# Linear attention plus routed feed-forward on one core: tiles 0 to 2 centred only, tiles 3 to 5 turned by TensorE, and the loads of x moved

## The chip, the cores and the metric

The kernel runs on one core of a Trainium2 chip. The metric is the device time of one execution in microseconds; before the change the median of three runs is 116.94 us (116.87 to 117.31). The engines are TensorE (PE, with PEld for its weight loads), VectorE (DVE), ScalarE (ACT), GpSimd (POOL) and SyncE (SP), whose queue issues most of the transfers. Every engine works through its own queue in the order in which the program was written out; they meet through semaphores.

## The reference

All arrays are bf16. x is 2048 tokens by 640.

```python
xn = _layernorm(x, axis=-1)
qkv = (xn @ wqkv)                       # 32 heads of 20
phi = lambda t: jnp.where(t > 0, t + 1, jnp.exp(t)) + 1e-6
kv = einsum("bhsd,bhse->bhde", phi(k), v);  z = phi(k) summed over s
o = (phi(q) @ kv) / (phi(q) . z + 1e-6)
A = o @ wo
r = xn @ w_r;  idx = argsort(-r)[:, :8]
y = (silu(xn[idx] @ w_gate) * (xn[idx] @ w_up)) @ w_down
B = xn, with y * sigmoid(r[idx]) added at the rows idx
return x + A + B
```

So the first thing that every token needs is its layer norm, and k, q and the routing logit r are products of the normalized token.

## The kernel before

**Tiles.** The tokens are 16 tiles of 128 (tile t is `x_sb[:, t, :]`). The normalized tile `xn[:, t, :]` has tokens on the partitions. The products k and q contract over the 640 features, so they read the turned tile `xnT`, features on the partitions, in five chunks of 128 (`kc`). The value projection is not computed for each token: the kernel sums G = xn^T phi(k) over all tiles and multiplies by the value weights once at the end.

**One tile.** `ln_stats(t)` is two BN_STATS on halves of 320 columns (lines 162 and 165), one aggregate (166), then the reciprocal root. It is two small operations on POOL, an add (168) and a power (171); for tiles 0 and 1 it is instead two activations on ACT (175, 176). `ln_scale(t)` (180, VectorE) subtracts the mean and multiplies by the root. Turning is done either by a DMA transpose issued from SP (`turn_dma`, 205), or by five TensorE transposes into a bank of PSUM (`turn_pe`, 192) and a copy out of it (`turned`, 200 on ACT or 202 on VectorE). `k_mm` (210) is ten matmuls in two halves of 320 columns; the second half has a 321st column, w_r, which gives the logit r. `k_act` (226 to 228, ACT) evicts exp, relu and the logit; `k_phi` (233, VectorE) makes phi(k) = min(exp, 1) + relu. `g_mm` (271) is five matmuls that add the tile to G.

**q.** Twenty units of 128 features by 512 tokens: `q_mm` (244), `q_act` (256, 257), `q_phi` (263). Units 0 to 4 read the turned tiles 0 to 3, units 5 to 9 the tiles 4 to 7.

**Order.** It is written out by hand and kept. SP loads the x of tiles 0 to 3 first, ACT's queue the k weights in two halves (122: chunks 0 to 2, 124: chunks 3 and 4). A memset on POOL (147) into two columns of x 4 holds back the loads after it: x 4 to 5, x 6 to 7, the q weights, x 8 to 9. Eight matmuls on zeros (291) come first on TensorE, one more later. Tiles 0 to 2 are turned by TensorE (tile 2 with VectorE's copy), tiles 3 to 15 by DMA. Each is scaled before it is turned. The x of tiles 10 to 15 is loaded in three pairs, each ahead of one DMA transpose. The column of w_r is turned by TensorE (319) and copied by ACT into `wk_sb` (320) in the middle of the k matmuls of tile 0.

**Loop.** From t = 3 to 15 a pass has k of tile t, q of unit t - 3 and G of tile t - 1 on TensorE. On VectorE it has phi of q for unit t - 4, the scaling of tile t + 3, the statistics of tile t + 4, some adds of xn to x in later passes (9 to 15), and phi of k for tile t. On POOL it has the root of tile t + 4 and one piece of the constants (`const_piece`). On SP it has the transpose of tile t + 3 and the loads of the later weights (`pieces`). After the loop come the top 8 tokens and their feed-forward, the product of the state with the output weights, the remaining q units, and the output; the change leaves all that as it is.

**Waits to know.** A transfer takes one of eight semaphores in turn, so its issue also waits for the transfer eight before it. PSUM banks 0 to 4 belong to G from its first tile on, banks 5 and 6 to k in the loop, and bank 7 to q.

## Time and profile before

| what | value |
|---|---|
| median of three runs | 116.94 us |
| the profiled execution, its own time | 117.29 us |
| its span, first to last instruction | 115.6 us |
| PE busy | 106.8 us (92%), 914 matmuls |
| VectorE busy | 83.9 us (73%) |
| ACT busy | 64.7 us (56%) |
| POOL busy | 34.3 us (30%) |
| moved by DMA | 22.20 MB, 192 GB/s on the mean |
| granted TensorE clock | 0.999 |

The times before and after are those of the whole execution; a span lies a little below. In the rows of the order of time, the first number is the start in us from the start of the span, the second the length, then the engine and the line of the kernel, what is written and what is read, and in brackets how long the engine was idle before it and what ended that. In the chain that ended last, each row is a start, a length and what the time was spent in.

### The profile page before, as it was taken

The page shows a single profiled execution, that of the slowest core. Times are in us where ns is not written, and L with a number is a line of the kernel's source. Part 1 is how long each engine was busy: PE and PEld are TensorE (multiplying, and loading weights), DVE is VectorE, ACT ScalarE, POOL GpSimd, SP SyncE. Part 2 cuts the span into 40 slices and gives each one's busy share as a digit, 9 for nine tenths or more (in the row PEclk, how much of TensorE's full clock was granted, in tenths as well). Part 3 has the DMA queues.
Part 4 walks back from the last instruction along what each step waited for, and adds up shares of the span by engine and source line. Part 5 has one row for each costly group of instructions (what it writes and reads, how often), then busy time and mean ns, then how long its engine had stood idle before and what let it go on. Part 6 is the DMA issues. An engine that isn't in the chain of part 4 may idle for free.

```text
span 115.6 us, 2496 instructions
## 1 busy us (share of the span) xinstructions
PE 106.8 (92%) x914; PEld 63.2 (55%) x922; DVE 83.9 (73%) x178; ACT 64.7 (56%) x127; POOL 34.3 (30%) x85
## 2 busy tenths in 40 slices
PE   5989996999999999999999998889799999999990
PEld 2445452555555555555555687644445666677770
DVE  0767999599998899877988976534537668695571
ACT  1558735655687555785556648896599465400000
POOL 7305357838777674500000005400060000000000
PEclk9999999999999999999999999999999999999999
DMA  3999279905998999999764995000003696984333
GB/s 95 318 381 338 60 176 161 234 2 109 281 231 228 223 368 223 347 322 243 290 227 149 257 384 186 0 0 6 0 1 72 173 330 155 317 289 169 113 113 113
DMA packets 23814, 22.20 MB, mean 192 GB/s; under 512 B 10074, under 2 KB 22522, under 8 KB 23802
## 3 DMA queue, kind: packets, MB, share of 16 engines
q1 hardware_dynamic: 21824, 19.99, 61.9%
q10 hardware_dynamic: 1834, 2.02, 5.1%
q0 software_dynamic: 144, 0.04, 0.6%
q8 instruction: 7, 0.11, 0.4%
q14 instruction: 5, 0.04, 0.1%
HBM read 14.62 MB, written 5.28 MB: 172 GB/s over the span
## 4 chain that ended last, share of the span: by engine, by line
PE 50%; DMA 15%; issue 13%; DVE 10%; POOLq 3%; SPq 3%; ACTq 1%; ACT 1%; POOL 1%; DVEq 0%
PE ps L210 16%; PE ps L271 11%; PE ps L244 11%; PE ps L756 11%; DMA wk_sb<-in_A_wqkv_dram 5%; DMA xnT<-xn 4%; DMA x_sb<-xxd 3%; DMA xxd<-y_sb,idxw 3%; POOLq L593 3%; SPq L740 3%; DVE xn L766 1%; DVE pk L233 1%; ACT spw L787 1%; DVE st L165 1%; DVE st L162 1%
## 5 line engine op out<-in xcount | busy, mean ns | idle before, releaser
L210 PE MATMUL ps<-wk_sb,xnT 128*128 128x320 bf16 (+1 forms) x160 | 25.2, 300 | 1.6 <-DMA xnT<-xn 1.1
L244 PE MATMUL ps<-xnT,wq_sb 128*128 128x512 bf16 x94 | 23.7, 379 | 0.5 <-issue 0.3
L756 PE MATMUL ps<-late,pqT 128*128 128x320 bf16 (+2 forms) x165 | 22.6, 295 | 0.0
L226 ACT ACTIVATE ek<-ps 128x640 bf16<-128x640 f32 x16 | 11.3, 704 | 19.0 <-PE ps L210 19.0
L210 PEld LDWEIGHTS <-xnT 128*128 128x128 bf16 x160 | 15.3, 98 | 11.0 <-DMA xnT<-xn 1.9
L271 PE MATMUL ps<-pk,xn 128*128 128x512 bf16 x78 | 19.8, 379 | 0.3 <-DVE pk L233 0.2
L263 DVE SCALAR_TENSOR_TENSOR pqT<-eq,rq 128x512 bf16<-128x512 bf16 x20 | 14.2, 709 | 8.0 <-ACT rq L257 7.9
L756 PEld LDWEIGHTS <-pqT 128*128 128x128 bf16 x165 | 15.6, 98 | 6.6 <-issue 0.6
L766 DVE TENSOR_TENSOR xn<-ps,x_sb 128x640 bf16<-128x640 f32 (+3 forms) x18 | 13.1, 748 | 5.5 <-PE ps L756 5.1
L233 DVE SCALAR_TENSOR_TENSOR pk<-ek,rk 128x640 bf16<-128x640 bf16 x16 | 13.3, 831 | 3.6 <-ACT rk L227 3.4
L244 PEld LDWEIGHTS <-wq_sb 128*128 128x128 bf16 x100 | 9.4, 97 | 9.5 <-issue 0.5
L256 ACT ACTIVATE eq<-ps 128x512 bf16<-128x512 f32 x20 | 12.3, 618 | 1.5 <-PE ps L244 1.5
L271 PEld LDWEIGHTS <-xn 128*128 128x128 bf16 x80 | 7.7, 98 | 9.5 <-issue 0.5
L257 ACT ACTIVATE rq<-ps 128x512 bf16<-128x512 f32 x20 | 12.3, 616 | 0.0
L171 POOL TENSOR_TENSOR rs<-rs,half 128x1 f32<-128x1 f32 x14 | 11.1, 793 | 1.1
L227 ACT ACTIVATE rk<-ps 128x640 bf16<-128x640 f32 x16 | 11.2, 697 | 0.0
L162 DVE BATCH_NORM_STATS2 st<-x_sb 128x6 f32<-128x320 bf16 x16 | 7.7, 479 | 3.6 <-DMA x_sb<-in_A_x_dram 3.6
L168 POOL TENSOR_TENSOR rs<-mv,half 128x1 f32<-128x1 f32 x14 | 5.4, 388 | 15.6 <-DVE mv L166 15.5
L594 POOL COPY xsT<-xnT 128x5 bf16 x8 | 3.0, 383 | 22.7 <-DVE gbf L672 20.5
L180 DVE TENSOR_SCALAR xn<-x_sb,mv,rs 128x640 bf16<-128x640 bf16 x16 | 7.7, 484 | 0.7 <-ACT rs L176 0.7
L165 DVE BATCH_NORM_STATS2 st<-x_sb 128x6 f32<-128x320 bf16 x16 | 7.6, 475 | 0.0
L787 ACT CAST spw<-ps 128x1024 bf16<-128x1024 f32 x5 | 4.9, 1014 | 3.7 <-PE ps L552 2.5
(121 smaller groups left out, 105.5 us busy)
## 6 DMA issues: line engine op xcount, KB each, us to landing
x_sb<-in_A_x_dram SPq DMA_DIRECT2D x6, 320.0 KB, 4.1
wg_sb<-in_B_w_gate_dram SPq DMA_DIRECT2D x5, 384.0 KB, 5.4
wu_sb<-in_B_w_up_dram SPq DMA_DIRECT2D x5, 384.0 KB, 4.1
wd_sb<-in_B_w_down_dram SPq DMA_DIRECT2D x3, 640.0 KB, 8.1
xxd<-x_sb SPq DMA_DIRECT2D x2, 640.0 KB, 3.2
out_dram<-xn SPq DMA_DIRECT2D x8, 160.0 KB, 2.1
x_sb<-xxd SPq DMA_DIRECT2D x2, 640.0 KB, 4.8
out_dram<-xn ACTq DMA_DIRECT2D x7, 160.0 KB, 2.2
```

Of the source, the lines that this page charges most:

```text
L171: nc.gpsimd.tensor_tensor(out=rs[:, 1:2], in0=rs[:, 0:1], in1=half[:, 1:2], op=ALU.pow)
L210: nc.tensor.matmul(ps[:, b + h, 0:w], lhsT=xnT[:, kc, t * P : (t + 1) * P], rhs=wk_sb[:, kc, h * HW : h * HW + w], start=(kc == 0), stop=( ...
L226: nc.scalar.activation(e[:], ps[:, b : b + 2, 0:HW], AF.Exp)
L227: nc.scalar.activation(r[:], ps[:, b : b + 2, 0:HW], AF.Relu)
L233: nc.vector.scalar_tensor_tensor(out=pk[:, t, :].rearrange("p (b f) -> p b f", b=2), in0=e[:], scalar=1.0, in1=r[:], op0=ALU.min, op1=ALU.add,
L244: nc.tensor.matmul(ps[:, b, :], lhsT=wq_sb[:, kc, m * P : (m + 1) * P], rhs=xnT[:, kc, tb * TBLK : (tb + 1) * TBLK], start=(kc == 0), stop ...
L256: nc.scalar.activation(e[:], ps[:, b, :], AF.Exp)
L257: nc.scalar.activation(r[:], ps[:, b, :], AF.Relu)
L263: nc.vector.scalar_tensor_tensor(out=pqT[:, m, tb * TBLK : (tb + 1) * TBLK], in0=e[:], scalar=1.0, in1=r[:], op0=ALU.min, op1=ALU.add,)
L271: nc.tensor.matmul(ps[:, c, :], lhsT=xn[:, t, c * P : (c + 1) * P], rhs=pk[:, t, 0:512], start=(t == 0), stop=(t == T - 1),)
L756: nc.tensor.matmul(ps[:, b, 0 : c1 - c0], lhsT=pqT[:, kc, t * P : (t + 1) * P], rhs=M_sb[:, kc, c0:c1], start=(kc == 0), stop=(kc == KC - 1),)
L766: nc.vector.tensor_tensor(out=xn[:, t, c0:c1].rearrange("p (b f) -> p b f", f=w), in0=ps[:, b : b + n, 0:w], in1=x_sb[:, t, c0:c1].rearran ...
```

## The change

The tiles 0, 1 and 2 are only centred before they are turned (`ln_centre`, subtracting the mean). The copies put them into unused parts of `GT` (`cT`), k is computed from them, and the factor 1/std of each token is applied by ACT as the row scale of the three evictions in `k_act`. For q and G the same tiles are scaled in place later (`ln_scale_centred`) and turned once more, by DMA. All roots come from POOL. Tiles 3, 4 and 5 are scaled as before, but turned by TensorE with ACT's copies in place of a DMA transpose. The warm-up matmuls are six in place of eight plus one.

The load of x 3 is issued behind a memset that follows the first POOL select; the loads of x 4 to 9 and the q weights are issued behind POOL's root of tile 0; x 10 to 15 is issued in one place, after the transposes of tiles 0 to 2. The w_r column is turned first on TensorE, copied by ACT to `wrT`, and put into `wk_sb` by POOL; tile 0 takes its logit from `wrT` by five matmuls of one column. The prologue is written out further, to the q units 0 and 1 and the scaling of tile 7, and the loop begins at t = 5. There the constants' pieces start two passes later, and two weight loads are issued in a pass from the start. The statistics' pool has five buffers in place of four.

```diff
@@ -25,7 +25,8 @@
 FJ = F // 4
 YW = D // 4
 EPS_BF16 = 1.0013580322265625e-05
-N_WARM = 8
+N_WARM = 6
+CENTRED = 3
 
 BF16 = mybir.dt.bfloat16
 F32 = mybir.dt.float32
@@ -64,7 +65,7 @@
 
     big = ctx.enter_context(tc.tile_pool(name="big", bufs=1))
     small = ctx.enter_context(tc.tile_pool(name="small", bufs=1))
-    lnp = ctx.enter_context(tc.tile_pool(name="lnp", bufs=4))
+    lnp = ctx.enter_context(tc.tile_pool(name="lnp", bufs=5))
     evk = ctx.enter_context(tc.tile_pool(name="evk", bufs=2))
     evq = ctx.enter_context(tc.tile_pool(name="evq", bufs=2))
     psum = ctx.enter_context(tc.tile_pool(name="ps", bufs=1, space=bass.MemoryType.PSUM))
@@ -103,6 +104,7 @@
     xsT = sb([P, KC, H], BF16, "xsT")
     maskkv = sb([EB, 5, DB], BF16, "maskkv")
     wr_rows = sb([KC, P], BF16, "wr_rows")
+    wrT = sb([P, KC], BF16, "wrT")
     r_all = sb([P, T], BF16, "r_all")
     kvT = sb([EB, NB, DB], BF16, "kvT")
 
@@ -122,7 +124,6 @@
     nc.scalar.dma_start(wk_sb[:, 0:3, 0:D], wqkv_v[:, 0:3, D : 2 * D])
     nc.sync.dma_start(x_sb[:, 2, :], x_v[:, 2, :])
     nc.scalar.dma_start(wk_sb[:, 3:KC, 0:D], wqkv_v[:, 3:KC, D : 2 * D])
-    nc.sync.dma_start(x_sb[:, 3, :], x_v[:, 3, :])
     nc.scalar.preload_act_table_set("natural_log_exp_and_others")
 
 
@@ -132,28 +133,36 @@
     nc.gpsimd.memset(half[:, 1:2], -0.5)
     nc.gpsimd.memset(grep[:], 1.0)
 
-    def grep_rows(j):
+    def grep_rows(j, then=None):
         g = grep[32 * j : 32 * j + 32, :]
         nc.gpsimd.affine_select(
             out=g, in_=g, compare_op=ALU.is_ge, fill=0.0, base=0,
             pattern=[[1, D]], channel_multiplier=-DH,
         )
+        if then is not None:
+            then()
         nc.gpsimd.affine_select(
             out=g, in_=g, compare_op=ALU.is_ge, fill=0.0, base=DH - 1,
             pattern=[[-1, D]], channel_multiplier=DH,
         )
 
-    grep_rows(0)
-    nc.gpsimd.memset(x_sb[:, 4, 0:2], 0.0)
-    nc.sync.dma_start(x_sb[:, 4:6, :], x_v[:, 4:6, :])
-    nc.sync.dma_start(x_sb[:, 6:8, :], x_v[:, 6:8, :])
-    nc.sync.dma_start(wq_sb[:], wqkv_v[:, :, 0:D])
-    nc.sync.dma_start(x_sb[:, 8:10, :], x_v[:, 8:10, :])
+    def late_x3():
+        nc.gpsimd.memset(x_sb[:, 3, 0:2], 0.0)
+        nc.sync.dma_start(x_sb[:, 3, :], x_v[:, 3, :])
+
+    def late_x4():
+        nc.gpsimd.memset(x_sb[:, 4, 0:2], 0.0)
+        nc.sync.dma_start(x_sb[:, 4:6, :], x_v[:, 4:6, :])
+        nc.sync.dma_start(x_sb[:, 6:8, :], x_v[:, 6:8, :])
+        nc.sync.dma_start(wq_sb[:], wqkv_v[:, :, 0:D])
+        nc.sync.dma_start(x_sb[:, 8:10, :], x_v[:, 8:10, :])
+
+    grep_rows(0, late_x3)
 
 
     stat = {}
 
-    def ln_stats(t, parts="abr", root="P"):
+    def ln_stats(t, parts="ab"):
         if "a" in parts:
             st = lnp.tile([P, 2, nc.vector.BN_STATS_DIM], F32, tag="st", name=f"st{t}")
             mv = lnp.tile([P, 2], F32, tag="mv", name=f"mv{t}")
@@ -164,16 +173,25 @@
             st, mv, rs = stat[t]
             nc.vector.bn_stats(out=st[:, 1, :], in_=x_sb[:, t, HW:D])
             nc.vector.bn_aggr(out=mv[:], in_=st[:])
-            if root == "P":
-                nc.gpsimd.tensor_tensor(
-                    out=rs[:, 0:1], in0=mv[:, 1:2], in1=half[:, 0:1], op=ALU.add
-                )
-                nc.gpsimd.tensor_tensor(
-                    out=rs[:, 1:2], in0=rs[:, 0:1], in1=half[:, 1:2], op=ALU.pow
-                )
-            else:
-                nc.scalar.activation(rs[:, 0:1], mv[:, 1:2], AF.Ln, bias=half[:, 0:1])
-                nc.scalar.activation(rs[:, 1:2], rs[:, 0:1], AF.Exp, scale=-0.5)
+            nc.gpsimd.tensor_tensor(
+                out=rs[:, 0:1], in0=mv[:, 1:2], in1=half[:, 0:1], op=ALU.add
+            )
+            nc.gpsimd.tensor_tensor(
+                out=rs[:, 1:2], in0=rs[:, 0:1], in1=half[:, 1:2], op=ALU.pow
+            )
+
+    def ln_centre(t):
+        _, mv, _ = stat[t]
+        nc.vector.tensor_scalar(
+            out=xn[:, t, :], in0=x_sb[:, t, :], scalar1=mv[:, 0:1], scalar2=None,
+            op0=ALU.subtract,
+        )
+
+    def ln_scale_centred(t):
+        _, _, rs = stat[t]
+        nc.vector.tensor_scalar(
+            out=xn[:, t, :], in0=xn[:, t, :], scalar1=rs[:, 1:2], scalar2=None, op0=ALU.mult
+        )
 
     def ln_scale(t):
         _, mv, rs = stat.pop(t)
@@ -193,9 +211,15 @@
                 psb(b)[:, kc * P : (kc + 1) * P], xn[:, t, kc * P : (kc + 1) * P], ident[:]
             )
 
+    def cT(t):
+        return GT[:, 1 + t, :].rearrange("p (k f) -> p k f", f=P)
+
     def turned(t, b, eng, c0=0, c1=KC):
         src = psb(b)[:, c0 * P : c1 * P].rearrange("p (k f) -> p k f", f=P)
-        dst = xnT[:, c0:c1, t * P : (t + 1) * P]
+        if t < CENTRED:
+            dst = cT(t)[:, c0:c1, :]
+        else:
+            dst = xnT[:, c0:c1, t * P : (t + 1) * P]
         if eng == "A":
             nc.scalar.copy(dst, src)
         else:
@@ -205,11 +229,14 @@
         nc.sync.dma_start_transpose(xnT[:, :, t * P : (t + 1) * P], xn[:, t, :])
 
 
-    def k_one(t, b, kc, h):
-        w = HW + h
+    def k_lhs(t, kc):
+        return cT(t)[:, kc, :] if t < CENTRED else xnT[:, kc, t * P : (t + 1) * P]
+
+    def k_one(t, b, kc, h, w=None):
+        w = w or HW + h
         nc.tensor.matmul(
             ps[:, b + h, 0:w],
-            lhsT=xnT[:, kc, t * P : (t + 1) * P],
+            lhsT=k_lhs(t, kc),
             rhs=wk_sb[:, kc, h * HW : h * HW + w],
             start=(kc == 0), stop=(kc == KC - 1),
         )
@@ -223,9 +250,16 @@
     def k_act(t, b):
         e = evk.tile([P, 2, HW], BF16, tag="ek", name=f"ek{t}")
         r = evk.tile([P, 2, HW], BF16, tag="rk", name=f"rk{t}")
-        nc.scalar.activation(e[:], ps[:, b : b + 2, 0:HW], AF.Exp)
-        nc.scalar.activation(r[:], ps[:, b : b + 2, 0:HW], AF.Relu)
-        nc.scalar.copy(r_all[:, t : t + 1], ps[:, b + 1, HW : HW + 1])
+        src, logit = ps[:, b : b + 2, 0:HW], ps[:, b + 1, HW : HW + 1]
+        if t < CENTRED:
+            rs = stat[t][2][:, 1:2]
+            nc.scalar.activation(e[:], src, AF.Exp, scale=rs)
+            nc.scalar.activation(r[:], src, AF.Relu, scale=rs)
+            nc.scalar.activation(r_all[:, t : t + 1], logit, AF.Copy, scale=rs)
+        else:
+            nc.scalar.activation(e[:], src, AF.Exp)
+            nc.scalar.activation(r[:], src, AF.Relu)
+            nc.scalar.copy(r_all[:, t : t + 1], logit)
         kbuf[t] = (e, r)
 
     def k_phi(t):
@@ -293,8 +327,12 @@
             )
 
     warm(N_WARM)
-    ln_stats(0, root="A")
-    ln_stats(1, "a")
+    ln_stats(0)
+    late_x4()
+    nc.tensor.transpose(psb(4)[:, 0:KC], wr_rows[:], ident[0:KC, 0:KC])
+    nc.scalar.copy(wrT[:], psb(4)[:, 0:KC])
+    ln_centre(0)
+    turn_pe(0, 7)
     for b in range(5):
         nc.tensor.matmul(
             ps[0:EB, 3, b * DB : (b + 1) * DB],
@@ -302,56 +340,86 @@
             rhs=grep[0:H, b * DB : (b + 1) * DB],
             start=(b == 0), stop=True, skip_group_check=True,
         )
+    turned(0, 7, "A", 0, 2)
+    turned(0, 7, "A", 2, KC)
     nc.scalar.copy(
         maskkv[:], ps[0:EB, 3, 0 : 5 * DB].rearrange("p (b f) -> p b f", b=5)
     )
-    ln_scale(0)
-    turn_pe(0, 7)
-    warm(1)
-    turned(0, 7, "A", 0, 2)
-    turned(0, 7, "A", 2, KC)
-    ln_stats(1, "b", root="A")
-    ln_stats(2, "a")
-    ln_scale(1)
-    ln_stats(2, "b")
+    nc.gpsimd.tensor_copy(wk_sb[:, :, D : D + 1], wrT[:].unsqueeze(2))
+    ln_stats(1)
+    ln_centre(1)
     for kc in range(3):
-        k_one(0, 5, kc, 0)
-    nc.tensor.transpose(psb(3)[:, 0:KC], wr_rows[:], ident[0:KC, 0:KC])
-    nc.scalar.copy(wk_sb[:, :, D : D + 1], psb(3)[:, 0:KC].unsqueeze(2))
+        for h in range(2):
+            k_one(0, 5, kc, h, HW)
+    turn_pe(1, 7)
     for kc in range(3, KC):
-        k_one(0, 5, kc, 0)
-    turn_pe(1, 4)
+        for h in range(2):
+            k_one(0, 5, kc, h, HW)
     for kc in range(KC):
-        k_one(0, 5, kc, 1)
-    turned(1, 4, "A", 0, 2)
-    turned(1, 4, "A", 2, KC)
+        nc.tensor.matmul(
+            ps[:, 6, HW : HW + 1], lhsT=k_lhs(0, kc), rhs=wrT[:, kc : kc + 1],
+            start=False, stop=(kc == KC - 1), skip_group_check=True,
+        )
+    turned(1, 7, "A", 0, 2)
+    turned(1, 7, "A", 2, KC)
+    ln_stats(2)
+    ln_centre(2)
+    k_act(0, 5)
+    k_mm(1, 2, 0, 4)
+    turn_pe(2, 4)
+    k_mm(1, 2, 4)
+    turned(2, 4, "A", 0, 2)
+    turned(2, 4, "V", 2, KC)
+    ln_scale_centred(0)
+    turn_dma(0)
+    ln_scale_centred(1)
+    turn_dma(1)
+    k_act(1, 2)
     ln_stats(3)
-    ln_scale(2)
-    k_act(0, 5)
-    k_mm(1, 2, 0, 6)
-    turn_pe(2, 7)
-    turned(2, 7, "V")
-    k_mm(1, 2, 6)
-    k_act(1, 2)
     k_phi(0)
+    k_mm(2, 5)
     ln_scale(3)
-    turn_dma(3)
-    ln_stats(4)
-    k_mm(2, 5)
+    g_mm(0)
     k_act(2, 5)
     k_phi(1)
+    ln_scale_centred(2)
+    turn_dma(2)
+    for t0 in (10, 12, 14):
+        nc.sync.dma_start(x_sb[:, t0 : t0 + 2, :], x_v[:, t0 : t0 + 2, :])
+    turn_pe(3, 7)
+    turned(3, 7, "A", 0, 2)
+    turned(3, 7, "A", 2, KC)
+    g_mm(1)
+    ln_stats(4)
+    k_phi(2)
+    ln_scale(4)
+    k_mm(3, 5)
+    turn_pe(4, 7)
+    turned(4, 7, "A", 0, 2)
+    turned(4, 7, "A", 2, KC)
     ln_stats(5)
-    ln_scale(4)
-    nc.sync.dma_start(x_sb[:, 10:12, :], x_v[:, 10:12, :])
-    turn_dma(4)
-    g_mm(0)
-    k_phi(2)
-    g_mm(1)
+    k_act(3, 5)
+    g_mm(2)
+    ln_scale(5)
+    k_phi(3)
+    q_mm(0, 7)
     ln_stats(6)
-    ln_scale(5)
-    nc.sync.dma_start(x_sb[:, 12:14, :], x_v[:, 12:14, :])
-    turn_dma(5)
-    nc.sync.dma_start(x_sb[:, 14:16, :], x_v[:, 14:16, :])
+    ln_scale(6)
+    turn_dma(6)
+    q_act(0, 7)
+    k_mm(4, 5)
+    q_phi(0)
+    k_act(4, 5)
+    turn_pe(5, 7)
+    turned(5, 7, "A")
+    g_mm(3)
+    ln_stats(7)
+    k_phi(4)
+    ln_scale(7)
+    turn_dma(7)
+    q_mm(1, 7)
+    q_act(1, 7)
+    ln_stats(8)
 
     def const_piece(i):
         if i == 0:
@@ -431,25 +499,22 @@
 
 
     added = 0
-    for t in range(3, T):
+    for t in range(5, T):
         k_mm(t, 5)
-        if t >= 4:
-            q_phi(t - 4)
-        if t == 3:
-            ln_stats(7)
+        q_phi(t - 4)
         if t + 3 < T:
             ln_scale(t + 3)
             turn_dma(t + 3)
-        if 3 < t < T - 4:
+        if t + 4 < T:
             ln_stats(t + 4)
         for _ in range(ADDS.get(t, 0)):
             add_xn(added)
             added += 1
-        const_piece(t - 3)
-        if t >= 5:
-            for _ in range(2 if t > 6 else 1):
-                if len(pieces) > 3:
-                    pieces.pop(0)()
+        if t < 12:
+            const_piece(t - 5)
+        for _ in range(2):
+            if len(pieces) > 3:
+                pieces.pop(0)()
         if t in STORES:
             store_xx(*STORES[t])
         k_act(t, 5)
```

## The prediction

> **What bounds the kernel now.** I read the busy times by stretch first, then the waits, the chain that ended last, and the order of time of the first 20 us.
>
> ```profile
> 10.00:20.00 10.00, 8.60 (x51) 4.57 (x52) 9.42 (x23) 5.53 (x13) 5.30 (x11) 1.00 0.70 163
> 20.00:28.00 8.00, 7.95 (x48) 4.58 (x47) 6.25 (x13) 4.69 (x10) 5.23 (x12) 1.00 0.52 110
> ...
> PE ps L210 <- DMA xnT<-xn: 1.1, 1, 1.1
> ```
>
> The columns are the stretch, its length, then busy PE, PEld, DVE, ACT and POOL. From 20 us TensorE is busy without a gap. Before that VectorE is the full one: 9.42 of 10 us. The one long TensorE wait is 1.1 us for the turned tile 4. The chain says whose lateness that is:
>
> ```profile
> 1.83 5.82 DMA wk_sb<-in_A_wqkv_dram
> ...
> 8.13 0.28 PE ps L192 x5
> ...
> 13.74 0.40 DVE st L162
> 14.15 0.40 DVE st L165
> ...
> 14.57 0.21 DVE mv L166
> 14.78 0.31 DVE xn L180
> 15.12 4.55 DMA xnT<-xn
> ...
> 19.72 1.56 PE ps L210 x10
> 21.27 1.08 PE ps L244 x5
> 22.35 1.08 PE ps L271 x5
> 23.43 1.38 PE ps L210 x10
> ```
>
> First the weights (second half landed at 1.83 + 5.82 = 7.65), then VectorE's queue up to the scaling of tile 4, then its DMA transpose. From 19.72 a pass costs 1.38 (k) + 1.08 (q) + 1.08 (G) = 3.54 us, all TensorE. So only what moves the loop's start, or makes VectorE late inside it, counts; the tail is unchanged and follows.
>
> **What VectorE's steps cost.** Rows in order of time (start, length, engine, line):
>
> ```profile
> 4.04 0.21 DVE L166 BATCH_NORM_AGGREGATE mv<-st 128x2 f32<-128x12 f32 x1
> 4.92 0.45 DVE L180 TENSOR_SCALAR xn<-x_sb,mv,rs 128x640 bf16<-128x640 bf16 x1 [0.31 <-ACT rs L176]
> 6.17 0.75 ACT L200 COPY xnT<-ps 128x256 bf16<-128x256 bf16 x2 [0.28 <-PE ps L192]
> 6.60 0.69 PE L210 MATMUL ps<-wk_sb,xnT 128*128 128x320 bf16 x3 [0.17 <-ACT xnT L200]
> 9.95 0.45 PE L192 MATMUL ps<-ident,xn 128*128 128x128 bf16 x5
> 10.44 0.49 DVE L202 COPY xnT<-ps 128x640 bf16<-128x640 bf16 x1 [0.55 <-PE ps L192]
> 12.85 0.21 DVE L166 BATCH_NORM_AGGREGATE mv<-st 128x2 f32<-128x12 f32 x1
> 12.97 0.77 DVE L233 SCALAR_TENSOR_TENSOR pk<-ek,rk 128x640 bf16<-128x640 bf16 x1
> 13.21 0.59 POOL L168 TENSOR_TENSOR rs<-mv,half 128x1 f32<-128x1 f32 x1 [2.63 <-DVE mv L166]
> 13.87 0.55 POOL L171 TENSOR_TENSOR rs<-rs,half 128x1 f32<-128x1 f32 x1
> 16.45 0.70 ACT L226 ACTIVATE ek<-ps 128x640 bf16<-128x640 f32 x1 [2.52 <-PE ps L210]
> 16.66 0.21 DVE L166 BATCH_NORM_AGGREGATE mv<-st 128x2 f32<-128x12 f32 x1
> 16.95 0.28 POOL L168 TENSOR_TENSOR rs<-mv,half 128x1 f32<-128x1 f32 x1 [0.71 <-DVE mv L166]
> 17.30 0.55 POOL L171 TENSOR_TENSOR rs<-rs,half 128x1 f32<-128x1 f32 x1
> 18.44 0.82 DVE L233 SCALAR_TENSOR_TENSOR pk<-ek,rk 128x640 bf16<-128x640 bf16 x1
> 18.65 1.02 POOL L171 TENSOR_TENSOR rs<-rs,half 128x1 f32<-128x1 f32 x1
> 19.18 0.69 DVE L263 SCALAR_TENSOR_TENSOR pqT<-eq,rq 128x512 bf16<-128x512 bf16 x1
> 29.27 1.24 PE L271 MATMUL ps<-pk,xn 128*128 128x512 bf16 x5
> ```
>
> A tile's statistics, start to next start: 0.40 + 0.40 + 0.02 + 0.08 until the pipe is empty, 0.12 for the aggregate (12.85 to 12.97) = 1.02 us. Phi of k: 0.73 to the next start (18.44 to 19.18). Phi of q: 0.69 long, 0.61 to the next by the same overlap of 0.08. A scaling: 0.31 (14.78 to 15.09) before a phi; I take 0.36 before statistics, 0.45 less the overlap.
>
> The reciprocal root on POOL is the important one. Alone, it runs from 16.66 + 0.21 = 16.87 to 17.30 + 0.55 = 17.85: **0.98 us** after the aggregate. With a phi behind the statistics the add, started at 13.21, ends at 13.80, just after that phi (12.97 + 0.77 = 13.74), and the root comes at 14.42, **0.68 after the phi's end**. The power at 18.65 was held likewise, past the phi that ended at 19.26. So POOL's small operations do not finish while VectorE streams a two-input operation.
>
> Before, nearly no scaling waits for this: the loop scales tile t + 3 one pass after its statistics, and the prologue puts statistics 5 ahead of scaling 4.
>
> **The change, part by part.**
>
> *Start of tile 0.* Centring (as the scaling, 0.45) starts at the aggregate's end, 4.25, instead of 4.92: tile 0 moves up 0.67. The first k matmul goes from 6.60 to about 5.94. It lies under the weights: the last four need the second half.
>
> *Weights and x of tile 3.* The issue of x 3 moves behind a POOL select and memset, from 2.18 to about 3.45. Its packets came behind those of tile 2:
>
> ```profile
> L125 SPq DMA_DIRECT2D x_sb<-in_A_x_dram x1: 432/432/432, 2.2 to 2.2; - x1
> DMA to landing us min/median/max: 5.2/5.2/5.2
> ...
> 4.11 0.39 SPq L148 DMA_DIRECT2D x_sb<-in_A_x_dram  x1
> ```
>
> It landed at 2.18 + 5.2 = 7.4, near the weights, so little clears their way; the x of tiles 4 and 5, now behind POOL's root of tile 0 (5.4 instead of 4.11), frees some more. Bounds for the landing: 7.65 (nothing gained) and 6.9 (the 160 KB of x 3 and some of x 4 out of the way). I take 7.3. The loads of x 4 to 9 and wq slip by 1.4 us; their readers (statistics 4 at 14, q of unit 0 at 18) have more room than that.
>
> *Logit by itself for tile 0*: five one-column matmuls, which the trace does not show; between nothing and the 0.138 of a 320-column matmul each; I take 0.06, by the nearest row (a 128-column transpose, 0.28 by five), 0.3 in all. The row-scale operand in three k evictions of each of three tiles costs ACT nothing to 0.7 (a second eviction pass) each; I take 0.1, and ACT waited 19 us in all for those matmuls:
>
> ```profile
> ACT ek L226 <- PE ps L210: 19.0, 15, 2.5
> ```
>
> *PE.* k of tile 0 ends at 7.35 + 4 x 0.138 + 0.3 = 8.2, four of tile 1 at 8.75, the transposes of tile 2 (5 in 0.45) at 9.2. Only then may VectorE copy its share: it starts at **9.24**, where it used to copy at 10.44. 1.2 us are gained here.
>
> *VectorE from there* does three scalings more than before (in place, tiles 0 to 2), less 0.23 of copy, and now has each scaling right behind its own statistics, with at most a phi between. The queue, in the new order:
>
> copy 0.26, scale 0 and 1 0.72: 10.22. Statistics 3: 11.24. Phi 0, whose place also holds the root: 0.82 + 0.69 + 0.03 = 1.54, 12.78. Scale 3, phi 1, scale 2 (0.31 + 0.73 + 0.36): 14.18. Statistics 4 and phi 2 with the held root: 16.74. Scale 4 and statistics 5: 18.12. Bare root (0.98, plus 0.09 as the aggregate is 0.21 long and counted with 0.12): 19.19. Scale 5: 19.55. Then phi 3 waits for ACT: transposes of tile 4 after scale 4 (17.18) end at 17.69, their copies take 0.75 and the k eviction of tile 3 behind them two of 0.70 with 0.1 overlapped, so 19.8; phi 3: 20.53. Statistics 6, bare root: 22.62. Scale 6, phi of q 0: 23.54. Statistics 7, phi 4 with held root: 26.10. Scale 7, statistics 8: 27.48. Phi of q 1 with held root (0.69 + 0.69 + 0.03): 28.89. Scale 8, statistics 9: 30.27. Phi 5 ends at **31.09**.
>
> G of tile 5 needs phi 5: it starts at 31.14, and started at 29.27. That is **+1.87**. The 1.2 us of head start is eaten by five to six exposed roots of 0.7 to 1.0 us and 1.1 us of scalings.
>
> *What is late next.* TensorE's pass is 3.54; VectorE's late pass is 1.02 + 0.73 + 0.61 + 0.36 and a root wait of about 0.5 = 3.2, so it would catch up by 0.3 a pass, but
>
> ```profile
> 27.77 0.72 POOL L137 TENSOR_SCALAR_AFFINE_SELECT grep<-grep 32x640 bf16<-32x640 bf16 x1
> ...
> 27.84 0.84 DVE L180 TENSOR_SCALAR xn<-x_sb,mv,rs 128x640 bf16<-128x640 bf16 x1
> ```
>
> the constants' selects (three passes, now two passes later) lengthen a scaling by 0.4, and from pass 9 the adds bring 0.36. It stays late over passes 6 to 11, and I estimate one more wait of 0.3. Sum: 1.87 + 0.3 = **+2.2 us**.
>
> *Hidden at no cost.* DMA transposes of tiles 0 to 2 are issued at 10, 11 and 14.3; even at 4.55 to landing the last is there at 18.9, against q of unit 0 at 18.6, before a later wait. The six x tiles issued together go ahead of the transpose of tile 6 on SP, but by 17.3, and that transpose waits until 23 for scaling 6. The column of w_r, copied by POOL after both weight halves, holds the roots of tiles 1 and 2 to 9.5; scalings 1 and 2 come at 9.9 and 13.8. A deeper statistics pool costs nothing.
>
> The profiled execution (117.29 around a span of 115.6) lies 0.35 above the median; I add to the median: 116.94 + 2.2 = **119.1**, span near 117.8.
>
> **The rivals.**
>
> *TensorE-bound start, VectorE keeps up.* Then k starts 0.66 earlier and the wait of 1.1 goes, against three more sets of transposes (3 x 0.28) and 0.3 of logits: 1.14. That gives -0.62: 116.3. The wait row speaks for it, the 9.42 of 10 us against. Chance 0.09.
>
> *The root is not held.* If each came 0.98 after its aggregate, the three held phis would cost 1.07 instead of 1.54 and the phi of q 0.34 less: 1.75 less, +0.45, 117.4. Against it are the two held rows. [...] Chance 0.10.
>
> *The clock comes late.*
>
> ```profile
> 1.38 3.59 PE L291 MATMUL ps<-GT 128*128 128x512 bf16 x8 [1.38 <-POOL GT L129]
> 5.93 0.50 PE L291 MATMUL ps<-GT 128*128 128x512 bf16 x1
> ```
>
> Eight warm matmuls took 0.43 each, later ones of that shape 0.216; full rate came around 6 us. The change drops three and leaves TensorE idle for some 0.7 us around 4.4. [...] For it: the idle time. [...] Chance 0.09.
>
> *Holding x 3 does nothing* for the weights: landing at 7.65, +0.35 on the sum, 119.5. It belongs to the forecast's own range, 118.5 to 120.
>
> **Numbers.** Forecast 0.70, unheld root 0.10, late clock 0.09, TensorE-bound 0.09, the rest others. Within 0.5% (116.36 to 117.52, about what a measurement here can tell) lies the unheld root: 0.10; slower 0.81; faster 0.09. The range of 117.1 to 120.8 takes in the unheld root and the late clock and leaves out the fast rival.
>
> **What would show it.** VectorE idle ahead of the scalings of tiles 3 to 8, released by POOL's root, 0.7 to 1.1 us each; phi 5 ending near 31, G of tile 5 waiting for it; TensorE idle ahead of the transposes of tile 4 by about 0.8; the weights near 7.3. I am wrong if the loop's k of tile 6 starts before 26.8, or if those waits are there and G of tile 5 is not late.

## The result, and the profile after

The changed kernel took 121.2 us as the median of four executions (120.12 to 122.24), beside 117.02 us (116.87 to 117.31) for the kernel before on the same chip. The ratio is 1.0284, 95% interval 1.0248 to 1.032, which puts the change at +3.3 us against the +2.2 of the forecast; two of the five executions, the profiled one of 122.24 us among them, came out at 122 us and are not in that ratio, and what sets them apart is found below.

The waits of the profiled execution of the changed kernel, each with its total in us, how often, and the longest:

```profile
DVE xn L198 <- POOL rs L179: 7.5, 12, 1.0
DVE GT L226 <- ACT GT L224: 3.9, 1, 3.9
PE ps L305 <- DVE pk L267: 1.7, 3, 1.0
PEld L237 <- DMA xnT<-xn: 1.5, 2, 0.8
```

The first row is the forecast's mechanism: twelve scalings on VectorE now wait 7.5 us for POOL's root, where nearly none did. The second was not in the forecast: VectorE's copy of tile 2 waits for a copy by ACT.

The busy times by stretch (stretch, length, busy PE, PEld, DVE, ACT, POOL, granted clock, DMA share, GB/s):

```profile
10.00:20.00 10.00, 8.17 (x56) 4.79 (x54) 7.00 (x17) 5.65 (x13) 2.41 (x4) 1.00 0.63 163
20.00:28.00 8.00, 7.32 (x45) 4.08 (x44) 5.27 (x13) 5.93 (x13) 2.58 (x6) 1.00 0.38 118
```

From 10 to 20 us VectorE fell from 9.42 of 10 to 7.00 and is late all the same: its idle time is waiting. TensorE, which was busy for 7.95 of 8 us from 20 to 28, is busy for 7.32.

The order of time of the same execution, where the two waits stand (start, length, engine, line, and in brackets the idle time before and what ended it):

```profile
4.69 0.71 PE L210 MATMUL ps<-ident,xn 128*128 128x128 bf16 x5 [0.46 <-DVE xn L185]
...
6.01 1.76 PE L237 MATMUL ps<-wk_sb,GT 128*128 128x320 bf16 x6
...
7.08 0.20 POOL L348 COPY wk_sb<-wrT 128x5 bf16<-128x5 bf16 x1 [1.69 <-DMA wk_sb<-in_A_wqkv_dram]
...
9.58 0.79 ACT L256 ACTIVATE ek<-ps,rs 128x640 bf16<-128x640 f32 x1 [0.49 <-PE ps L359]
...
10.37 0.67 PE L210 MATMUL ps<-ident,xn 128*128 128x128 bf16 x5
10.95 0.26 ACT L258 ACTIVATE r_all<-ps,rs 128x1 bf16<-128x1 f32 x1
11.09 0.38 ACT L224 COPY GT<-ps 128x256 bf16<-128x256 bf16 x1
11.50 0.36 DVE L226 COPY GT<-ps 128x384 bf16<-128x384 bf16 x1 [3.89 <-ACT GT L224]
...
13.41 0.77 DVE L267 SCALAR_TENSOR_TENSOR pk<-ek,rk 128x640 bf16<-128x640 bf16 x1
13.57 0.66 POOL L176 TENSOR_TENSOR rs<-mv,half 128x1 f32<-128x1 f32 x1 [4.73 <-DVE mv L175]
14.31 0.55 POOL L179 TENSOR_TENSOR rs<-rs,half 128x1 f32<-128x1 f32 x1
14.89 0.45 DVE L198 TENSOR_SCALAR xn<-x_sb,mv,rs 128x640 bf16<-128x640 bf16 x1 [0.71 <-POOL rs L179]
...
20.08 0.21 DVE L175 BATCH_NORM_AGGREGATE mv<-st 128x2 f32<-128x12 f32 x1
20.43 0.19 POOL L176 TENSOR_TENSOR rs<-mv,half 128x1 f32<-128x1 f32 x1 [1.66 <-DVE mv L175]
20.70 0.55 POOL L179 TENSOR_TENSOR rs<-rs,half 128x1 f32<-128x1 f32 x1
21.29 0.45 DVE L198 TENSOR_SCALAR xn<-x_sb,mv,rs 128x640 bf16<-128x640 bf16 x1 [1.00 <-POOL rs L179]
...
33.11 1.24 PE L305 MATMUL ps<-pk,xn 128*128 128x512 bf16 x5 [0.48 <-DVE pk L267]
```

Three things are to be seen. First, the held root: the add of 13.57 takes 0.66 us and ends at 14.23, just after the phi that ended at 13.41 + 0.77 = 14.18, and the scaling follows 0.71 after the phi's end. The bare root, without a phi, takes 0.19 + 0.55 and ends at 21.25, 0.96 after its aggregate's end. Second, the copy of line 226 starts at 11.50, behind ACT's share of the same tile (11.09 to 11.47), though the transposes that it reads ended at 10.37 + 0.67 = 11.04; and in ACT's queue that share stands behind the three evictions of tile 0, which end at 11.21. Third, the k matmuls of tile 0 run at about half rate: six in 1.76 us, where the rows of before give 0.138 each, 0.83 for six. This is the forecast's late clock; the granted clock of the profile reads 1.00 from 4 to 10 us all the same, so the name rests on the lengths of the matmuls. G of tile 5 starts at 33.11; before it was 29.27.

### The profile page after: what moved, and what is told of

It reads as the page before. It is cut to its first block, busy times and chain, and to the rows that moved or that the text cites. A ratio compares the mean times of both kernels' runs of the same rounds, so it can differ in the third digit from the quotient of the medians.

```text
span 120.5 us, 2554 instructions
## 1 busy us (share of the span) xinstructions
PE 110.1 (91%) x939; PEld 65.0 (54%) x939; DVE 83.9 (70%) x181; ACT 67.0 (56%) x129; POOL 36.2 (30%) x91
## 4 chain that ended last, share of the span: by engine, by line
PE 47%; DVE 19%; DMA 10%; ACT 9%; POOL 8%; issue 4%; ACTq 1%; DVEq 0%; POOLq 0%
PE ps L821 14%; PE ps L278 10%; PE ps L237 8%; DMA xnT<-xn 6%; PE ps L305 5%; POOL rs L179 5%; POOL rs L176 4%; DMA wk_sb<-in_A_wqkv_dram 4%; DVE xn L198 4%; ACT spw L634 3%; DVE st L171 3%; DVE st L174 3%; DVE xn L831 2%; DVE mv L175 1%; PE ps L314 1%
## 5 line engine op out<-in xcount | busy, mean ns | idle before, releaser
L278 PE MATMUL ps<-xnT,wq_sb 128*128 128x512 bf16 x100 | 24.4, 379 | 0.7 <-ACT xnT L224 0.7
L237 PE MATMUL ps<-wk_sb,xnT 128*128 128x320 bf16 (+1 forms) x130 | 20.1, 300 | 0.5 <-DMA xnT<-xn 0.3
L297 DVE SCALAR_TENSOR_TENSOR pqT<-eq,rq 128x512 bf16<-128x512 bf16 x20 | 13.7, 684 | 6.2 <-ACT rq L291 6.2
L260 ACT ACTIVATE ek<-ps 128x640 bf16<-128x640 f32 x13 | 9.2, 705 | 14.3 <-PE ps L237 14.3
L237 PEld LDWEIGHTS <-xnT 128*128 128x128 bf16 x130 | 12.6, 98 | 8.4 <-DMA xnT<-xn 1.5
L176 POOL TENSOR_TENSOR rs<-mv,half 128x1 f32<-128x1 f32 x16 | 7.8, 485 | 19.9 <-DVE mv L175 19.0
L267 DVE SCALAR_TENSOR_TENSOR pk<-ek,rk 128x640 bf16<-128x640 bf16 x16 | 12.8, 799 | 0.5 <-ACT rk L261 0.4
L261 ACT ACTIVATE rk<-ps 128x640 bf16<-128x640 f32 x13 | 9.1, 700 | 0.0
```

The lines of the kernel that those rows point to most:

```text
L176: nc.gpsimd.tensor_tensor(out=rs[:, 0:1], in0=mv[:, 1:2], in1=half[:, 0:1], op=ALU.add)
L237: nc.tensor.matmul(ps[:, b + h, 0:w], lhsT=k_lhs(t, kc), rhs=wk_sb[:, kc, h * HW : h * HW + w], start=(kc == 0), stop=(kc == KC - 1),)
L267: nc.vector.scalar_tensor_tensor(out=pk[:, t, :].rearrange("p (b f) -> p b f", b=2), in0=e[:], scalar=1.0, in1=r[:], op0=ALU.min, op1=ALU.add,
L278: nc.tensor.matmul(ps[:, b, :], lhsT=wq_sb[:, kc, m * P : (m + 1) * P], rhs=xnT[:, kc, tb * TBLK : (tb + 1) * TBLK], start=(kc == 0), stop ...
L297: nc.vector.scalar_tensor_tensor(out=pqT[:, m, tb * TBLK : (tb + 1) * TBLK], in0=e[:], scalar=1.0, in1=r[:], op0=ALU.min, op1=ALU.add,)
```

## The experiments

Ratios are to the kernel before, run beside each version on the same chip, with their 95% intervals; the rows of each kernel are from one profiled execution of it. I call "the start" what lies ahead of VectorE's copy of tile 2, "the prologue" what lies from there to G of tile 5, and "the loop" the rest up to the first matmul of the state's product (line 280 before, 314 after). That matmul started at 65.09 before, and what follows it is the same work.

### The changed kernel again, twice

Nothing is edited.

> The changed kernel once more, for a second trace. All theories: about 120.3. If TensorE reaches its full rate near 6 us in this execution (the k matmuls of tile 0 in pairs of 0.14 us instead of 0.27), VectorE's copy of tile 2 starts near 9.5 instead of 11.5, and G of tile 5 near 31.3 instead of 33.1; the waits of VectorE for POOL's root before the scalings stay at 0.7 to 1.0 us each.

Measured: 121.99 us (121.67 to 122.29), 1.0403 (1.0373 to 1.0433). That is above the 120.3 expected, and all four executions lie in the upper part of the first set's scatter. In the profiled one (122.29 us) the condition for the early start did not come: the first six k matmuls of tile 0 take 1.78, VectorE's copy starts at 11.48 and G of tile 5 at 33.10, as in the first profile, and the waits for a root are 7.5 us in all again.

> The changed kernel once more, with nothing edited, for its spread. Theory (a TensorE clock that comes late in some executions and in time in others): the times fall into two groups, near 120.3 and near 122, some 1.5 us apart; in the profiled execution the first six matmuls of k of tile 0 take about 1.76 us where the time is near 122, and 1.2 or less where it is near 120.3. Rival (the scatter comes from the loads): both kinds of execution run those matmuls at the same rate, and the weights' landing, near 7.05 otherwise, differs by a microsecond or more.

Measured: 121.4 us (120.7 to 122.38), 1.0368 (1.0306 to 1.043). The six times fall into two groups with nothing between: 120.70, 120.76, 120.97 and 121.83, 121.95, 122.38, whose means (120.81 and 122.05) differ by 1.24. This time the profiled execution is one of the lower group, 120.70 us. Its order of time:

```profile
4.72 0.45 PE L210 MATMUL ps<-ident,xn 128*128 128x128 bf16 x5 [0.49 <-DVE xn L185]
...
5.95 0.98 PE L237 MATMUL ps<-wk_sb,GT 128*128 128x320 bf16 x6 [0.47 <-DMA wk_sb<-in_A_wqkv_dram]
...
7.55 0.20 POOL L348 COPY wk_sb<-wrT 128x5 bf16<-128x5 bf16 x1 [2.14 <-DMA wk_sb<-in_A_wqkv_dram]
...
8.66 0.44 PE L210 MATMUL ps<-ident,xn 128*128 128x128 bf16 x5
...
9.72 0.27 ACT L258 ACTIVATE r_all<-ps,rs 128x1 bf16<-128x1 f32 x1
9.86 0.38 ACT L224 COPY GT<-ps 128x256 bf16<-128x256 bf16 x1
...
10.28 0.36 DVE L226 COPY GT<-ps 128x384 bf16<-128x384 bf16 x1 [1.77 <-ACT GT L224]
...
18.08 0.46 PE L210 MATMUL ps<-ident,xn 128*128 128x128 bf16 x5 [0.56 <-DVE xn L198]
...
31.05 0.77 DVE L267 SCALAR_TENSOR_TENSOR pk<-ek,rk 128x640 bf16<-128x640 bf16 x1
...
31.88 1.24 PE L305 MATMUL ps<-pk,xn 128*128 128x512 bf16 x5 [0.48 <-DVE pk L267]
...
36.09 0.93 DVE L198 TENSOR_SCALAR xn<-x_sb,mv,rs 128x640 bf16<-128x640 bf16 x1 [0.44 <-POOL rs L179]
36.13 0.71 POOL L138 TENSOR_SCALAR_AFFINE_SELECT grep<-grep 32x640 bf16<-32x640 bf16 x1
...
39.79 0.93 DVE L198 TENSOR_SCALAR xn<-x_sb,mv,rs 128x640 bf16<-128x640 bf16 x1 [0.45 <-POOL rs L179]
...
46.61 1.24 PE L305 MATMUL ps<-pk,xn 128*128 128x512 bf16 x5 [0.40 <-DVE pk L267]
...
68.42 1.74 PE L314 MATMUL ps<-pk,xn 128*128 128x128 bf16 x28
```

The five transposes of tile 0 take 0.45 here, the first six k matmuls 0.98, and the copy starts at 10.28, 1.22 before that of the execution of 122.24 us, although the weights landed later (7.55 against 7.08 by the column's copy). So it is TensorE's rate and not the loads that parts the two groups: the theory of the late clock holds, its rival fails. Here the wait of the copy is ACT's queue alone: the transposes end at 8.66 + 0.44 = 9.10, and ACT is at tile 0's evictions until 9.99.

### More warm-up matmuls

```diff
-N_WARM = 6
+N_WARM = 8
```

> One part undone: eight warm-up matmuls ahead of everything instead of six. Theory of the late clock: full rate near 6 us in every execution, so all executions lie together near 120.2. Rival (the warm-up does not matter): the same scatter between executions as the changed kernel has, 120 to 122.

Measured: 120.73 us (120.56 to 121.08), 1.0308 (1.0276 to 1.034), 1.26 under the changed kernel on the same chip. From the order of time:

```profile
6.20 1.20 PE L237 MATMUL ps<-wk_sb,GT 128*128 128x320 bf16 x6
7.24 0.44 PE L210 MATMUL ps<-ident,xn 128*128 128x128 bf16 x5
...
10.36 0.36 DVE L226 COPY GT<-ps 128x384 bf16<-128x384 bf16 x1 [2.02 <-ACT GT L224]
```

Full rate is there by 7.24. The upper group is gone from the four executions, which lie where the lower group lies: by these four, eight warm-ups make nothing quicker, they only keep the clock from coming late. The further kernels below that have eight warm-ups ran 18 times, and one execution (122.03 us, with VectorE's copy) again lies 2 us above its fellows; no trace of it was kept, so it is not shown whether its clock was late.

With seven:

> The changed kernel with seven warm-up matmuls in place of six. Theory (late clock): the idle stretch of TensorE near 4.4 us shrinks from about 0.5 to about 0.1, so the executions near 122 become rare, the median falls to 120.3 to 120.9 and the spread under 1 us. Rival (any start with fewer than eight is late): the spread and the median stay as with six, 120.1 to 122.3.

Measured: 121.91 us (120.68 to 122.23), 1.0365 (1.0301 to 1.0429). Four of six executions are in the upper group. The profiled one is among them:

```profile
4.81 0.71 PE L210 MATMUL ps<-ident,xn 128*128 128x128 bf16 x5 [0.15 <-DVE xn L185]
...
5.99 1.78 PE L237 MATMUL ps<-wk_sb,GT 128*128 128x320 bf16 x6
```

The expectation failed. TensorE is idle for only 0.15 us there, and the clock still comes late; the seventh matmul bought nothing that six executions can show, the eighth (which leaves no idle time before the transposes) did. Here the rival, that any start with fewer than eight is late in part of its executions, is the one that holds for the six and seven that were run.

### The pace of the weight loads in the loop

```diff
-        for _ in range(2):
+        for _ in range(2 if t > 6 else 1):
```

> One part undone: the loop issues one weight load in its passes 5 and 6 instead of two. Theory A (nearly all of the loss is the exposed roots): 0.2 us less at most. Theory B (about 1 us of it is the DMA transposes of tiles 10 and 11 landing behind the weight loads, 7 us after their issue): 0.7 to 1.0 us less, near 119.4, and no TensorE wait for a turned tile after 40 us.

Measured: 121.76 us (120.73 to 122.52), 1.0363 (1.031 to 1.0415), which can't be told from the unchanged 121.99. The suspicion came from the chain of waits of the first profile:

```profile
41.98 7.34 DMA xnT<-xn
49.37 1.56 PE ps L237 x10
```

A turned tile took 7.34 us to land, and k waited for it. In the edited kernel that wait is gone, but G of tile 9 then waits 0.41 for phi, as it does in the unedited kernel above (0.40 at 46.61). From G of tile 5 to the state's product the unedited kernel took 36.85 us in one execution (33.11 to 69.96) and 36.54 in another (31.88 to 68.42), the edited one 36.54. So the two loads per pass cost some 0.3 us in some executions, and nothing shows that they do so regularly.

### x of tile 3 not held back

```diff
+    nc.sync.dma_start(x_sb[:, 3, :], x_v[:, 3, :])
...
-    grep_rows(0, late_x3)
+    grep_rows(0)
```

It is the kernel with eight warm-ups, with the load of x 3 back at its old place.

> Eight warm-ups, and the load of x 3 issued with the first ones again, not behind the POOL select. Theory (its packets came behind those of x 2 anyhow): the same as with eight warm-ups alone, 120.7 within 0.3, and POOL's copy of the w_r column, which waits for both weight halves, within 0.3 us of where it was. Rival (holding x 3 brings the weights forward): the copy comes 0.5 us later and the time rises by as much.

Measured: 120.63 us (120.39 to 121.02), 1.0317 (1.0291 to 1.0343), against 1.0308 with the load held. POOL's copy of the column starts at 7.23, where it started at 7.40 with the load held. Holding it does nothing that can be measured for the time or the weights.

### VectorE copies tile 2 alone

```diff
-    turned(2, 4, "A", 0, 2)
-    turned(2, 4, "V", 2, KC)
+    turned(2, 4, "V")
```

Again with eight warm-ups.

> Eight warm-ups, and VectorE copies the whole turned tile 2 by itself instead of sharing the copy with ACT. Theory (VectorE's queue began late because its share waits for ACT's share, which stands behind the three evictions of tile 0): VectorE's copy starts near 9.2 instead of 10.36, everything behind it moves by about 1.0 us, and the time falls from 120.7 to about 119.7. Rival (the start of VectorE's queue does not set the end): 120.7.

Measured: 119.76 us (119.48 to 122.03), 1.0228 (1.0194 to 1.0262); by the ratios (1.0308 - 1.0228) x 117 = 0.94 us less than with eight warm-ups alone.

```profile
8.96 0.49 DVE L226 COPY GT<-ps 128x640 bf16<-128x640 bf16 x1 [0.80 <-PE ps L210]
...
18.62 1.24 PE L278 MATMUL ps<-xnT,wq_sb 128*128 128x512 bf16 x5 [0.18 <-DMA xnT<-xn]
...
30.72 1.24 PE L305 MATMUL ps<-pk,xn 128*128 128x512 bf16 x5 [0.20 <-DVE pk L267]
```

The copy now waits for TensorE's transposes alone and starts at 8.96 in place of 10.36, and G of tile 5 follows at 30.72 in place of 31.97. The wait for ACT is what the forecast's start of VectorE lacked.

### Statistics one tile ahead

```diff
     k_phi(0)
+    ln_stats(4)
     k_mm(2, 5)
...
-    ln_stats(4)
+    ln_stats(5)
     k_phi(2)
...
     k_phi(4)
     ln_scale(7)
...
-    ln_stats(8)
```

The statistics of tiles 4 to 8 are each written one place earlier, so that VectorE has other work while POOL makes the root. The rest is the changed kernel, with six warm-ups.

> VectorE's order alone: the statistics of tiles 4 to 8 each move one tile ahead, so that a whole tile's statistics (1.02 us, during which POOL is not held) lie between the statistics and the scaling of a tile; nothing else changes. Theory A (exposed roots): VectorE's waits for POOL before the scalings of tiles 4 to 7 fall from 0.7-1.0 us to under 0.1, and the time falls by 1.6 us, to about 118.7. Rival (VectorE's three additional scalings or the weight loads are what costs): within 0.3 us of the changed kernel.

Measured: 119.77 us (118.71 to 120.22), 1.0192 (1.0139 to 1.0245), 2.2 us under the changed kernel on the same chip. In its profiled execution the clock was late (the first six k matmuls of tile 0 take 1.76) and VectorE's copy started at 11.70, later than in any trace above but one, yet G of tile 5 starts a microsecond before the 33.10 of the unedited kernel on that chip:

```profile
32.12 1.24 PE L305 MATMUL ps<-pk,xn 128*128 128x512 bf16 x5
```

From there to the state's product it takes 35.82 (32.12 to 67.94), as the kernel before does (29.27 to 65.09), where the unedited kernel took 36.54 or more: the other microsecond comes in the loop. In the whole kernel these waits for a root are left, in the groups by line (busy and mean ns, then idle before and its releaser):

```profile
L198 DVE TENSOR_SCALAR xn<-x_sb,mv,rs 128x640 bf16<-128x640 bf16 x13 | 6.8, 527 | 1.3 <-POOL rs L179 1.3
```

7.5 us of waiting became 1.3, and 2.2 us of the time went with it. This shows the forecast's mechanism by an edit: the statistics, roots and scalings are the same, and only their order is another. The rival's three additional scalings and the weight loads are still there.

### Both, and tile 5 turned by DMA again

First eight warm-ups, VectorE's copy and the order of statistics together:

> Eight warm-ups, VectorE's copy of tile 2 by itself, and the statistics one tile ahead. If late clock, late start and exposed roots are separate costs that add up, about 117.7: 120.7 less 1.0 less 2.0. If they hide each other, above 118.5.

Measured: 118.82 us (118.76 to 119.28), 1.0163 (1.0134 to 1.0192). By the ratios that is 0.0065 x 117 = 0.76 less than without the order, where 2.0 was expected: the costs overlap. G of tile 5 starts at 30.73, and it started at 30.72 without the order. All of the gain thus comes in the loop, which takes 35.82 in place of 36.54 (30.72 to 67.26); ahead of G of tile 5 the exposed roots no longer come last, and two waits of TensorE do.

```profile
18.99 1.24 PE L278 MATMUL ps<-xnT,wq_sb 128*128 128x512 bf16 x5 [0.97 <-ACT r_all L262]
...
23.65 1.24 PE L278 MATMUL ps<-xnT,wq_sb 128*128 128x512 bf16 x5 [0.68 <-ACT xnT L224]
...
66.55 1.74 PE L314 MATMUL ps<-pk,xn 128*128 128x128 bf16 x28
```

The product of the state starts 66.55 - 65.09 = 1.46 late, and these two waits of TensorE are 1.65. The first is put down to ACT's copy of a logit, but the q matmul does not wait for that one: the program lets it wait for ACT's copies of tiles 3 and 4 (done at 17.73) and for the second turning of tiles 0 to 2. The last of those was issued at 14.31. In the trace its semaphore gets the last update at 18.86, and TensorE's sequencer passes its wait for that semaphore at 18.89, 0.1 ahead of q. In the kernel with VectorE's copy alone the last second turning was issued at 13.99 and landed 4.49 later, at 18.48, and q starts at 18.62, before that logit is copied (19.21), so it does not wait for the logit. The second wait is for ACT's copy of tile 5, which stands behind the evictions of tile 4.

Then tile 5 by DMA as before, which takes the second wait away:

```diff
     ln_scale(5)
+    turn_dma(5)
...
-    turn_pe(5, 7)
-    turned(5, 7, "A")
```

> Eight warm-ups, VectorE's copy of tile 2, statistics one tile ahead, and tile 5 turned by DMA again. Theory (what is left of the loss is TensorE's wait of 0.68 us for ACT's copy of tile 5, behind the k eviction of tile 4, and the transposes themselves): 0.9 less than with tile 5 on TensorE, about 117.9. Rival (the left loss lies at q of unit 0, which waits for the second turning of tile 2 by DMA, and moves only there): 118.8.

Measured: 118.2 us (117.69 to 118.33), 1.0079 (1.0046 to 1.0112): 0.62 less by the medians and 0.98 by the ratios, around the 0.9 expected.

```profile
19.36 0.81 PE L278 MATMUL ps<-xnT,wq_sb 128*128 128x512 bf16 x3 [1.01 <-ACT r_all L262]
```

The wait of 0.68 is gone, that of 1.01 for the second turning of tile 2 remains (issued at 14.64, landed at 19.22, the wait for it passed at 19.25), and the product starts at 65.80, 0.71 late. What no edit took away is thus the second turning itself. A kernel without it was not tried.

### One part alone, in the kernel before

Only tile 4 is turned by TensorE, in the middle of the k matmuls of tile 3, and copied by ACT; all else is as before.

```diff
-    turn_dma(4)
...
-        k_mm(t, 5)
+        k_mm(t, 5, 0, 4 if t == 3 else 10)
+        if t == 3:
+            turn_pe(4, 7)
+            turned(4, 7, "A", 0, 2)
+            turned(4, 7, "A", 2, KC)
+            k_mm(t, 5, 4)
```

> The kernel before with one part of the change alone: tile 4 turned by TensorE, in the middle of the k matmuls of tile 3, with ACT's copies, in place of its DMA transpose. Theory (that transpose was the one late thing before the loop, 1.14 us, and ACT stands idle there): k of tile 4 starts near 18.9 instead of 19.72 and the time falls by 0.8, to about 116.3. Rival (VectorE's queue or the next DMA transpose is late next): within 0.3 of 117.1.

Measured over ten executions: 116.5 us (116.23 to 118.49) beside 117.13, ratio 0.9955 (0.9922 to 0.9989). It is the only version that beats the kernel before, by about half a microsecond.

```profile
15.42 0.44 PE L192 MATMUL ps<-ident,xn 128*128 128x128 bf16 x5
15.70 0.99 PE L210 MATMUL ps<-wk_sb,xnT 128*128 128x320 bf16 x6
...
18.86 1.55 PE L210 MATMUL ps<-wk_sb,xnT 128*128 128x320 bf16 x10
```

Five transposes cost TensorE 0.28 us (15.42 to 15.70), the wait of 1.14 for the turned tile is gone, and k of tile 4 starts at 18.86 in place of 19.72. The state's product starts 0.86 earlier too, at 64.23, a little more than the 0.5 to 0.6 that the median times show.

### Fewer warm-ups in the kernel before

```diff
-N_WARM = 8
+N_WARM = 6
...
-    warm(1)
```

> The kernel before with six warm-ups and without the single one behind the transposes of tile 0; nothing else. Theory of the late clock: the k matmuls of tile 0 run at 0.27 us each, and the time rises by 0.8 to 1.5 us, with more scatter. Rival (three warm-ups do not matter, the clock came late for another reason): 117.0.

Measured: 117.99 us (117.48 to 119.56), 1.0049 (0.9995 to 1.0102): the interval includes 1, and the scatter is hardly wider than that of the kernel before on the same chip (116.87 to 118.74), so the expected loss of 0.8 to 1.5 is not shown. Its profiled execution, of 119.08 us, shows something that the others don't:

```profile
6.43 0.62 PE L210 MATMUL ps<-wk_sb,xnT 128*128 128x320 bf16 x3 [0.54 <-DMA wk_sb<-in_A_wqkv_dram]
...
8.40 0.69 PE L210 MATMUL ps<-wk_sb,xnT 128*128 128x320 bf16 x2 [1.25 <-DMA wk_sb<-in_A_wqkv_dram]
8.88 0.74 PE L192 MATMUL ps<-ident,xn 128*128 128x128 bf16 x5
```

Full rate was there early (three k matmuls in 0.62). After a further wait for weights, of 1.25 us, it was lost again (five transposes in 0.74); TensorE had also waited 0.83 us ahead of the transposes of tile 0 and 0.54 ahead of k.

## Why the prediction came out as it did

The direction and the mechanism were right, and the time (120.3 by the ratio) lies in the range; the sum was 1.1 us short of it. That the time lies in the range is in part luck. Of the fifteen executions of the changed kernel five lie in it, one at 120.97, and the nine with the late clock near 122; the ratios of the two repeats, 1.0403 and 1.0368, give about 121.7 and 121.3 on 117. Taken by its own steps, against the execution of 120.70 us, in which the clock was in time and which is 3.41 over the profiled one of before:

- **Weights near 7.3.** Right: the column's copy, which waits for them, starts at 7.08 to 7.55 in the traces. Holding x 3 was priced as perhaps useless, and it is (7.23 without it), so the number did not come from holding x 3; what brought it from 7.65 stays open.
- **Transposes of tile 2 end at 9.2.** Right: 8.66 + 0.44 = 9.10.
- **"Only then may VectorE copy its share: it starts at 9.24".** Wrong, and the largest miss: 10.28. The step asked only what the copy reads. It also waits for ACT's share of the same tile, and ACT's queue had the evictions of tile 0 in front of it. That is +1.04, and moving the whole copy to VectorE brought 0.94 of time back.
- **VectorE's queue from the copy to phi 5.** Right in size: 21.85 us forecast (9.24 to 31.09), 21.54 measured (10.28 to 31.05 + 0.77 = 31.82). It holds step by step too: the scaling of tile 4 was put 7.50 behind the copy's start and came 7.30 behind it, that of tile 8 19.65 and 19.38. The held root was put at 0.68 after the phi's end and came at 0.71; the bare one at 0.98 and came at 0.96. G of tile 5 at 31.88 in place of 31.14 is the missed wait less the 0.3 that the queue was quicker. Taking the roots out of the way is worth 2.2 us in the changed kernel and 0.76 with the start mended, since the other waits move up.
- **"One more wait of 0.3" in the loop.** Too small: from G of tile 5 to the state's product the delay grows from 31.88 - 29.27 = 2.61 to 68.42 - 65.09 = 3.33, so by 0.72. The pass of VectorE was put at 3.2 us, with 0.4 more for the passes with selects; those passes came to 3.70 (0.93 for the scaling, and 0.44 for a root in every pass), above TensorE's 3.54, so VectorE fell further back where the forecast had it nearly hold. With the statistics one tile ahead the loop takes no longer than before the change, so it is the root in each pass that makes VectorE late there.
- **The sum.** 2.2 + 1.04 - 0.31 + 0.42 = 3.35, and the state's product is 3.33 late.
- **TensorE idle 0.8 ahead of tile 4's transposes.** It was 0.56 in the traces of the unedited kernel.
- **"Hidden at no cost": the second turning of tiles 0 to 2.** Right for the changed kernel, in which VectorE is later still, but only as long as that is so: with the other delays mended TensorE waits 1.01 for it, and the state's product is 0.71 late. The row scale on ACT was put at 0.1 an eviction, and the rows give 0.79 against 0.70.

Of the rivals, the **TensorE-bound start** did not come, since VectorE was late. The **unheld root** is refuted by the held adds (0.66 in place of 0.19, ending 0.05 after the phi). The **late clock** had a chance of 0.09 and, by the times near 122, came in nine of fifteen executions of the changed kernel: 2 of 5, 4 of 4 and 3 of 6. The range's upper end of 120.8 was set to take it in, by a delay of full rate that no run shows; what the runs showed is 1.24 between the two groups, times near 122, above that end, and in the execution of 122.24 us five transposes at 10.37 that still took 0.67. So it should have stood beside the forecast as an even chance, and not as a remote one. What spoke for it was TensorE's idle time; yet with seven warm-ups 0.15 us of idle time went with the late clock, and in the execution of 120.70 us 0.49 went with the early one. What parts the two groups of one unchanged program, and how much idle time TensorE's rate bears, was not shown: these runs give the cases, not the limit.

## What to carry to other kernels

Look at all that the program makes an operation wait for, and not only at what it reads: here VectorE's copy of tile 2 started at 10.28, though the transposes that it reads had ended at 9.10. Where one copy is split between two engines, one share can be made to wait for the other (1.77 us in that execution, 3.89 in that of 122.24 us), so look at what stands in front of each; whether here the bank that both read or the buffer that both write is the reason was not tried. A small result that crossed to another engine and back, the bare root, came 0.96 after its aggregate; with the statistics of another tile written between its two ends VectorE's waits for it fell from 7.5 us to 1.3, and a change that moves work up to shorten a start must keep that distance. Before removing warm-up work from TensorE, look at the spread over executions and not at one trace: here the loss came in nine of fifteen.

## What the runs showed of the hardware

- With six warm-up matmuls TensorE's full rate came early or late in the same program: by 4.7 us in the execution of 120.70 us (transposes of tile 0 in 0.45), and past 8 us in those profiled near 122 (k of tile 0 at 1.76 to 1.78 for six; in that of 122.24 us the transposes of tile 2 still 0.67 at 10.37). With seven, the profiled execution (121.92 us) was late too (1.78). With eight, the transposes of tile 1 ran at full rate (0.44 at 7.24). The granted clock does not tell the two kinds apart: for 10 to 20 us it reads 1.00 in both, for 4 to 10 us 1.00 in the execution of 122.24 us, and in that of 120.70 us 0.9 or more in every slice of its profile. It is the length of the matmuls that does.
- A rate once granted was lost in a stretch in which TensorE never idled for longer than 1.25 us: in the kernel before with six warm-ups it waited 0.83 and 0.54, three k matmuls took 0.62, it waited 1.25, and then two took 0.69 and five transposes 0.74 in place of 0.44. There the granted clock fell with it: in tenths, 8 from 5.9 to 8.8 us and 5 from 8.8 to 11.7. The execution of 120.70 us, at full rate from 4.72, kept it over waits of 0.47, 0.23 and 0.37, and over one of 1.15 (G of tile 0 at 13.01, five matmuls in 1.24).
- A 128x1 add on POOL that took 0.19 us alone took 0.66 while a two-input operation of VectorE ran beside it, and ended 0.05 after that operation. In the kernel before, a power that took 0.55 beside the statistics took 1.02 from 18.65, and ended at 19.67: after the phi of k that ran until 19.26, but within the phi of q (19.18 to 19.87). VectorE's scaling in turn took 0.93 in place of 0.45 while POOL's select over 640 columns ran.
